# Issue positions of VectorE's weight merges, w_l and xl in the attention stage of a fused attention and gated-FFN kernel

## Chip, cores and metric

The kernel runs on one core of a Trainium2 chip. The metric is the device time of one execution in microseconds (us). An execution is taken apart by the hardware profiler; its engines are TensorE (PE for matmuls, PEld for weight loads), VectorE (DVE), ScalarE (ACT), GpSimd (POOL) and SyncE (SP), which here only issues DMAs.

## The reference

```
scores = (1/sqrt(64)) * q @ k.T          # B=4, H=12, S=448, D=64; causal mask
attn   = exp(scores - max) ; attn /= attn.sum + 1e-9
x      = (attn @ v) as 1792 x 768
xn     = x / sqrt(mean(x*x) + 1e-6) * rms_g
g, val = xn @ w_gate, xn @ w_val         # 768 x 1536 each
out    = (g * sigmoid(g) * val) @ w_out  # 1536 x 768
```

Everything is computed in float32 accuracy. Weights arrive as 64-bit floats and are turned into 32-bit ones on the chip.

## The kernel before

**Tiling.** The rows of x are cut into four groups: the first 256 queries of batches 0 and 1, those of batches 2 and 3, the next 128 queries of all batches and the last 64 (512, 512, 512 and 256 columns). The first group has 12 attention units (6 pairs of heads times two batches); its attention is the first stage, written out as rounds of six ticks. After it comes a loop over weight chunks `s` for each group: the FFN of one group runs while the attention of the next is threaded between its matmuls.

**A round of the first stage** (round r starts at tick 6r; `round_steps`, L425). Tick 0: the scores of unit r, eight matmuls (L180, called S), and four masked negated maxima on VectorE (L189). Tick 1: attn @ v of unit r-3 (L262, called AV) and its copy `xr` on VectorE (L271). Tick 2: the transposes of the first half of unit r-2 (L236, called T0), copied by ScalarE (`pt`, L242). Ticks 3 and 4: single FFN steps that are ready early (`ffn_part`, three matmuls L391 to L393: w_h times xh, w_h times xl, w_l times xh). Tick 5: the transposes of the second half (T1), copied by VectorE (`pt`, L240). At the end of tick 2 ScalarE's exponentials of unit r are issued (`exp0`), and at the end of tick 0 of the next round VectorE's reciprocal of the sums (L201) with GpSimd's four normalising multiplications (L197, `norm0`), which T0 and T1 read two rounds after the scores.

**Side work of the first stage.** `convert(s)` turns chunk s of the weights into 32 bits: ScalarE c0 (L352), GpSimd c1 (L353), VectorE c2 and c3 (L355 and L357, "the merges"), then a DMA that stores the chunk (L359). `split_w` makes w_h on ScalarE (L367) and w_l on VectorE (L369, even s) or GpSimd (L92, odd s). `split_x` makes xh on ScalarE (L306) and xl on VectorE (L307). `square` makes the squares and their sum `acc` on GpSimd (L92); the last sum goes through PE (`r_ps`, L314), ScalarE's root (L316) and VectorE's reciprocals (L319) into the FFN's first results.

**Order.** The schedule is written out by hand: each engine works through its instructions in the order in which the program issues them. `post(d, fn)` issues fn d ticks on, at the end of the tick before; `post(1, ...)` is the end of the same tick. `T` holds these delays, `LOAD`, `CONVERT` and `SPLIT` the ticks at which chunks are loaded, converted and split, `READY_W` and `READY_X` the ticks from which an early FFN step may be placed (only at ticks 3 and 4 of a round). What is posted for the same tick is issued in the order in which it was posted.

So before the change the VectorE queue around rounds 5 to 8 reads (max5 are the maxima of unit 5, pt3 the second copy of unit 3): `xr1 c2_0 pt2 c3_0 max5 rcp4 xr2 pt3 xl0 max6 rcp5 xr3 c2_1 wl0 pt4 c3_1 max7 rcp6 xr4 pt5 xl1 max8`.

Of the kernel before, what the change touches and what calls it, by code (L numbers as in the profile page):

```python
# [14 lines left out]
ALU = mybir.AluOpType  # L15
# [22 lines left out]
MASKED = -8.0e9  # L38


T = dict(c0=0, c1=1, c2=4, c20=9, c3=5, c30=10, c5=7, c50=14, exp=1, exp0=3, gt=1, hh=1, hl=4,
         ld=4, ld1=11, lv=5, norm0=7, norm1=2, r1=5, so=3, wl=2, wl0=8, xl=2, xl0=9)
LOAD = (4, 12, 24, 36, 48, 60, 74)
CONVERT = (20, 32, 44, 62, 76)
SPLIT = (33, 45, 57)

READY_W, READY_X = (45, 57, 68), (40, 52, 64, 76, 87)
WR = 4
WARM = [9, 0, 0, 2]
EXTRA = 4  # L50
# [5 lines left out]
def attention_ffn(ctx: ExitStack, tc: tile.TileContext, qk0, qk1, qk2, v, v2, w, g, out):  # L56
# [7 lines left out]
    nc = tc.nc  # L64
# [23 lines left out]
    def f32(ap):  # L88
        return ap.bitcast(F32)

    def pool_op(out_, a, op, b):
        nc.gpsimd.tensor_tensor(out_, a, b, op=op)  # L92
# [27 lines left out]
    def post(delay, fn):  # L120
        if delay <= 0:
            fn()
        else:
            later.setdefault(now[0] + delay, []).append(fn)
# [6 lines left out]
    xr, xh, xl, acc = {}, {}, {}, {}  # L131
# [6 lines left out]
    def load_qk(p):  # L138
        if p < len(UNITS):
            _, kind, _, _, row = UNITS[p]  # L140
            raw_qk[p] = raw.tile([P, 2, W], F32, tag="qk", name="qk_r")
            if kind == 2:
                nc.sync.dma_start(out=raw_qk[p], in_=qk2[row])
            else:
                nc.sync.dma_start(out=raw_qk[p][:, 0], in_=(qk0, qk1)[kind][row])
# [14 lines left out]
    def steps_s(p):  # L160
# [22 lines left out]
        def softmax(e, i, pss):  # L183
            o, wd = bl[i]
            ps, sp = pss[e][:, o: o + wd], pr["sp"][e][:, o: o + wd]
            n = len(bl) * e + i
            nm, sm, rs = (pr[m][:, n: n + 1] for m in ("nm", "sm", "rs"))
            mk = mask2 if kind == 2 else mask[:, 3 * P - wd:]
            nc.vector.tensor_tensor_reduce(  # L189
                out=sp, in0=ps, in1=mk, scale=nsc, scalar=3.0e38,  # L190
                op0=ALU.add, op1=ALU.min, accum_out=nm)
            post(T["exp" if p >= ENDS[0] else "exp0"], lambda: nc.scalar.activation(  # L192
                sp, sp, AF.Exp, bias=nm, scale=-1.0, accum_out=sm))
            if ENDS[0] + 3 <= p < ENDS[1]:
                pr["norms"].append(lambda: nc.scalar.mul(sp, sp, rs))
            else:
                pr["norms"].append(lambda: nc.gpsimd.tensor_scalar(  # L197
                    sp, sp, rs, 1.0, op0=ALU.mult, op1=ALU.mult))
# [6 lines left out]
        def step():  # L205
# [5 lines left out]
            for e in range(2):  # L211
                for i in range(len(bl)):
                    softmax(e, i, pss)
            post(T["exp" if p >= ENDS[0] else "exp0"], lambda: nc.scalar.activation(
                pr["sm"][:, :nb], pr["sm"][:, :nb], AF.Identity, bias=tiny))
            post(T["norm1" if kind else "norm0"], norm)
            post(2, lambda: load_qk(p + 4))
# [60 lines left out]
    def cols(b):  # L278
        return GROUPS[b][3]

    def square(b, c):
# [13 lines left out]
        if c == NP - 1:  # L295
            post(T["r1"], lambda: rms(b, acc[b]))
        waiting.append((b, c))

    def split_x():
        if not waiting:  # L300
# [5 lines left out]
        nc.scalar.mul(h, x, gc)  # L306
        post(T["xl0" if b == 0 and c < NP - 1 else "xl"], lambda: nc.vector.scalar_tensor_tensor(  # L307
            out=l, in0=x, scalar=gc, in1=f32(h), op0=ALU.mult, op1=ALU.subtract))
        xh[b, c], xl[b, c] = h, l

    def rms(b, sq):

        ps = ps_t.tile([P, W], F32, tag="t", name="r_ps")[:, : cols(b)]
        nc.tensor.matmul(ps, ones, sq, start=True, stop=True)  # L314
        r = rinv[b] = xx_p.tile([P, W], F32, tag="rms", name="rms", bufs=2)[:, : cols(b)]
        nc.scalar.activation(r, ps, AF.Sqrt, bias=eps, scale=1.0 / DM)  # L316
        for i in range(cols(b) // P):
            sl = slice(i * P, (i + 1) * P)
            nc.vector.reciprocal(r[:, sl], r[:, sl])  # L319
# [22 lines left out]
    def convert_ops(s):  # L342
        if s >= NU:
# [7 lines left out]
        return [  # L351
            (T["c0"], lambda: nc.scalar.mul(t, hf_, 2.0 ** -112)),  # L352
            (T["c1"], lambda: nc.gpsimd.tensor_scalar(  # L353
# [8 lines left out]
    def split_w(s):  # L362
        if s < NG * NU:
            t = wt[s]
            h = ws_p.tile([P, DM], F32R, tag="wh", name="w_h")
            l = ws_p.tile([P, DM], F32R, tag="wl", name="w_l")
            nc.scalar.copy(h, t)  # L367
            if s % 2 == 0 and (s < NU or cols(s // NU) < W):
                post(T["wl" if s > 1 else "wl0"], lambda: nc.vector.tensor_tensor(l, t, f32(h), op=ALU.subtract))  # L369
            else:  # L370
                post(T["wl"], lambda: pool_op(l, t, ALU.subtract, f32(h)))
            wt[s] = tuple(a.rearrange("p (k m) -> p k m", m=P) for a in (h, l))
# [75 lines left out]
    with tc.manual_schedule():  # L448
# [19 lines left out]

        for fs, at_ in ((load_w, LOAD), (lambda n: convert(n), CONVERT), (split_w, SPLIT)):
            for n, t_ in enumerate(at_):  # L470
                at_tick(t_, lambda fs=fs, n=n: fs(n))
# [13 lines left out]
        def convert(s):  # L485
            for d, op in convert_ops(s):
                post(d, op)
# [12 lines left out]
        for s in range(NG * NU):  # L500
            w_ = s // NU
            if s % NU == 0:
                at, goal = done, ends[w_ + 1] + 2 if w_ + 1 < NG else done
                if w_ + 2 == NG:
                    goal = ends[w_ + 1]
            if s + 7 < NU:
                post(T["ld"], lambda s=s: load_w(s + 7))
            if s + 6 >= NU:
                post(T["ld1"], lambda s=s: load_w(s + 6))
            for k0 in (0, 2, 4):  # L510
                ks = [k for k in (k0, k0 + 1) if (s, k) not in early]
                if ks:
                    ffn_part(s, ks)
                i = 3 * (s % NU) + k0 // 2 + 1
                while done < goal and (done - at) < (goal - at) * i / AT[w_]:
                    steps[done]()
                    done += 1
                if i >= 73:
                    split_x()
                if k0 == 0:  # L520
                    convert(s + 5)
                if k0 == (0 if s < 3 else 4):
                    split_w(s + 3)
                for fn in prep.pop(now[0], []):
                    fn()
                tick()
# [50 lines left out]
```

## Time and profile before

| | us |
|---|---|
| median of 3 runs | 722.12 (721.94 to 722.2) |
| the profiled execution, device time | 721.81 |
| its span, first to last instruction | 720.0 |
| PE busy in the span | 699.6 (97%) |
| VectorE, ScalarE, GpSimd busy | 418.6, 366.5, 415.0 |

The span begins at the first instruction. The first stage runs from about 5 us to about 68 us; from 75 us on PE has work nearly without a break. A row of a timeline gives start, duration, engine, source line, operation, output from input, shapes, and in brackets how long the engine was idle before it and what it waited for. Where consecutive operations of an engine overlap in their records, the distance from one start to the next is what an operation costs in a queue.

### The profile page before, as it was taken

To read this page: it belongs to the slowest core of one execution; us is meant where nothing else is said; L and a number is where in the kernel's file an instruction comes from. 1 tells how busy PE (TensorE), PEld (TensorE's weight loads), DVE (VectorE), ACT (ScalarE), POOL (GpSimd) and SP (SyncE) were. 2 spreads that over 40 slices of the span, in tenths; PEclk is the share of its full clock that TensorE was granted. 3 is DMA by queue.
4 is the path that set the end of the run, shared out by engine and by line. 5 is a ranking of instruction groups with operands and counts; after the bars stand their busy time and mean duration, and the time that the engine had idled before them with its cause. 6 is when DMAs were issued, how large, how long until landed. Compare 5 with 4: busy or idle time off the path is not lost.

```text
span 720.0 us, 11950 instructions
## 1 busy us (share of the span) xinstructions
PE 699.6 (97%) x4256; PEld 546.7 (76%) x4256; DVE 418.6 (58%) x857; ACT 366.5 (51%) x811; POOL 415.0 (58%) x349
## 2 busy tenths in 40 slices
PE   8778899999999999999999999999999999999998
PEld 6455667777777777777777777777777788899998
DVE  4976899999998454545454534234333442137752
ACT  6958777877856344434444444334344342235441
POOL 4988435466476454675576637266455563437763
PEclk9999999999999999999999999999999999999999
DMA  8746487778767433333334456353641423355553
GB/s 265 250 146 204 154 266 247 261 261 281 271 223 251 145 126 135 117 117 121 131 127 147 160 180 223 112 188 115 191 139 48 137 66 118 117 177 179 179 177 111
DMA packets 47307, 123.47 MB, mean 171 GB/s; under 512 B 5968, under 2 KB 12880, under 8 KB 47248
## 3 DMA queue, kind: packets, MB, share of 16 engines
q1 hardware_dynamic: 47248, 122.71, 51.5%
q8 instruction: 34, 0.56, 0.3%
q14 instruction: 25, 0.20, 0.1%
HBM read 103.03 MB, written 19.66 MB: 170 GB/s over the span
## 4 chain that ended last, share of the span: by engine, by line
PE 73%; DVE 11%; issue 5%; POOL 5%; ACT 4%; DMA 2%; POOLq 0%; DVEq 0%; ACTq 0%
PE m_ps L391 20%; PE m_ps L393 19%; PE m_ps L392 19%; PE av_ps L262 5%; PE s_ps L180 5%; PE t_ps L236 4%; DVE w L355 3%; POOL sp L197 2%; DVE w_c L357 2%; DMA w<-in_w 2%; DVE sp L189 2%; DVE w_l L369 1%; ACT sp L192 1%; POOL w L353 1%; ACT w_c L352 1%
## 5 line engine op out<-in xcount | busy, mean ns | idle before, releaser
L391 PE MATMUL m_ps<-xh,w_h 128*128 128x512 f32 (+1 forms) x576 | 221.7, 385 | 0.0
L92 POOL TENSOR_TENSOR w_l<-w_r,w_h 128x768 fp32r<-128x768 f32 x90 | 170.1, 1896 | 73.6 <-ACT w_h L367 45.1
L393 PE MATMUL m_ps<-xh,w_l 128*128 128x512 f32 (+1 forms) x576 | 210.6, 366 | 0.0
L392 PE MATMUL m_ps<-xl,w_h 128*128 128x512 f32 (+1 forms) x576 | 210.2, 365 | 0.0
L197 POOL TENSOR_SCALAR sp<-sp,rs 128x384 f32<-128x384 f32 (+3 forms) x132 | 84.0, 652 | 142.1 <-DVE rs L201 135.7
L192 ACT ACTIVATE sp<-sp,nm 128x128 f32<-128x128 f32 (+3 forms) x168 | 87.5, 524 | 71.7 <-DVE nm L189 71.2
L391 PEld LDWEIGHTS m_ps<-xh,w_h 128*128 128x128 f32 x576 | 109.2, 190 | 18.8 <-issue 3.8
L393 PEld LDWEIGHTS m_ps<-xh,w_l 128*128 128x128 f32 x576 | 109.0, 189 | 18.8
L367 ACT CAST w_h<-w_r 128x768 fp32r<-128x768 f32 x108 | 87.5, 826 | 64.2 <-DMA w_r<-w 39.9
L392 PEld LDWEIGHTS m_ps<-xl,w_h 128*128 128x128 f32 x576 | 109.5, 190 | 13.3
L391 PE MATMUL m_ps<-hh,w_h 128*128 128x512 f32 (+1 forms) x288 | 109.1, 379 | 0.0
L393 PE MATMUL m_ps<-hh,w_l 128*128 128x512 f32 (+1 forms) x288 | 105.0, 365 | 0.9 <-DVE w_l L369 0.9
L392 PE MATMUL m_ps<-hl,w_h 128*128 128x512 f32 (+1 forms) x288 | 104.8, 364 | 0.4 <-DVE hl L417 0.4
L240 DVE COPY pt<-t_ps 128x384 f32<-128x384 f32 (+1 forms) x84 | 49.8, 592 | 70.6 <-PE t_ps L236 70.5
L189 DVE CUSTOM_DVE_ANT_0 sp<-s_ps,mask 128x128 f32<-128x128 f32 (+3 forms) x168 | 67.2, 447 | 36.1 <-PE s_ps L180 34.5
L406 ACT ACTIVATE t_sb<-gr 128x512 f32<-128x512 f32 (+1 forms) x48 | 27.8, 578 | 110.5 <-DVE gr L405 110.5
L262 PEld LDWEIGHTS av_ps<-pt,v_r 128*64 128x64 f32 (+1 forms) x864 | 40.7, 137 | 48.3 <-issue 17.8
L262 PE MATMUL av_ps<-pt,v_r 128*64 128x128 f32 (+2 forms) x864 | 60.7, 269 | 11.8 <-DVE pt L240 6.7
L353 POOL TENSOR_SCALAR w<-w 128x768 f32<-128x768 f32 x36 | 44.0, 1223 | 42.1 <-ACT w_c L352 34.2
L236 PE MATMUL t_ps<-ident,sp 128*128 128x128 f32 (+1 forms) x384 | 63.0, 276 | 0.9 <-POOL sp L197 0.4
L393 PEld LDWEIGHTS m_ps<-hh,w_l 128*128 128x128 f32 x288 | 54.4, 189 | 10.3 <-DVE w_l L369 1.3
L236 PEld LDWEIGHTS t_ps<-ident,sp 128*128 128x128 f32 (+1 forms) x384 | 47.7, 138 | 18.7 <-POOL sp L197 3.0
(53 smaller groups left out, 878.5 us busy)
## 6 DMA issues: line engine op xcount, KB each, us to landing
w_r<-w SPq DMA_DIRECT2D x108, 384.0 KB, 3.8
w<-in_w SPq DMA_DIRECT2D x36, 768.0 KB, 5.1
w<-w_c SPq DMA_DIRECT2D x36, 384.0 KB, 2.8
qk_r<-in_qk SPq DMA_DIRECT2D x48, 256.0 KB, 3.1
qk_r<-in_qk SPq DMA_DIRECT2D x12, 512.0 KB, 3.6
v_r<-in_v SPq DMA_DIRECT2D x12, 448.0 KB, 6.1
out_t<-ob SPq DMA_DIRECT2D x18, 256.0 KB, 2.3
v_r<-in_v SPq DMA_DIRECT2D x24, 192.0 KB, 3.8
```

Of the source, the lines that this page charges most:

```text
L92: nc.gpsimd.tensor_tensor(out_, a, b, op=op)
L189: nc.vector.tensor_tensor_reduce(out=sp, in0=ps, in1=mk, scale=nsc, scalar=3.0e38, op0=ALU.add, op1=ALU.min, accum_out=nm)
L192: post(T["exp" if p >= ENDS[0] else "exp0"], lambda: nc.scalar.activation(sp, sp, AF.Exp, bias=nm, scale=-1.0, accum_out=sm))
L197: pr["norms"].append(lambda: nc.gpsimd.tensor_scalar(sp, sp, rs, 1.0, op0=ALU.mult, op1=ALU.mult))
L236: nc.tensor.transpose(ps[:kb, at: at + P], pr["sp"][e][:, o + kb * j: o + kb * (j + 1)], ident)
L240: nc.vector.tensor_copy(pt[:kb, :at], ps[:kb, :at])
L262: nc.tensor.matmul(av_ps[e * D: (e + 1) * D, p % 2, q0: q0 + n], raw_v[p][:kb, h, j, e, :], pr["pt", e][:kb, a0: a0 + n], start=(j == 0), ...
L353: (T["c1"], lambda: nc.gpsimd.tensor_scalar(hf_, hf_, 0.0, 1.0, op0=ALU.mult, op1=ALU.mult)),
L367: nc.scalar.copy(h, t)
L391: nc.tensor.matmul(ps, wh[:, k, :], mh, start=(first and k == ks[0]), stop=False)
L392: nc.tensor.matmul(ps, wh[:, k, :], ml, start=False, stop=False)
L393: nc.tensor.matmul(ps, wl[:, k, :], mh, start=False, stop=(last and k == 5))
```

## The change

The delays `c20` and `c30` of c2 and c3 (first five chunks) become 11 and 11 (from 9 and 10), that of the store `c50` 16 (from 14), that of w_l `wl0` 10 (from 8; it now also holds for chunk 2, which had `wl` = 2), that of xl `xl0` 10 (from 9). Chunk 4 is converted at tick 74 instead of 76, chunk 6 loaded at 76 instead of 74. READY_W moves by a tick for chunks 0 and 2; the early FFN steps keep their order. In the first stage c2, c3, w_l and xl are then all issued at the end of a tick 0, behind the maxima of that score step and ahead of the reciprocal posted for the same tick.

```
-T = dict(c0=0, c1=1, c2=4, c20=9, c3=5, c30=10, c5=7, c50=14, ...
-         ld=4, ld1=11, lv=5, norm0=7, norm1=2, r1=5, so=3, wl=2, wl0=8, xl=2, xl0=9)
-LOAD = (4, 12, 24, 36, 48, 60, 74)
-CONVERT = (20, 32, 44, 62, 76)
+T = dict(c0=0, c1=1, c2=4, c20=11, c3=5, c30=11, c5=7, c50=16, ...
+         ld=4, ld1=11, lv=5, norm0=7, norm1=2, r1=5, so=3, wl=2, wl0=10, xl=2, xl0=10)
+LOAD = (4, 12, 24, 36, 48, 60, 76)
+CONVERT = (20, 32, 44, 62, 74)
 SPLIT = (33, 45, 57)
-READY_W, READY_X = (45, 57, 68), (40, 52, 64, 76, 87)
+READY_W, READY_X = (46, 57, 69), (40, 52, 64, 76, 87)
...
-                post(T["wl" if s > 1 else "wl0"], lambda: nc.vector.tensor_tensor(l, t, f32(h), op=ALU.subtract))
+                post(T["wl" if s > 2 else "wl0"], lambda: nc.vector.tensor_tensor(l, t, f32(h), op=ALU.subtract))
```

The same stretch of the VectorE queue after the change: `xr1 pt2 max5 c2_0 c3_0 rcp4 xr2 pt3 max6 xl0 rcp5 xr3 pt4 max7 c2_1 c3_1 wl0 rcp6 xr4 pt5 max8 xl1`. Later in the stage: `max9 c2_2 c3_2 rcp8`, `max10 xl2 rcp9`, `max11 wl2 rcp10`, `max12 c2_3 c3_3 xl3 rcp11`, `max14 c2_4 c3_4 xl4 rcp13`. GpSimd's and PE's queues keep their order; on ScalarE c0 of chunk 4 and xh4 change places; on SP each store moves behind one load of v.

## Rows read from the trace of the kernel before

**Rows 1.** Stretches: length, busy us of PE, PEld, DVE, ACT, POOL; clock; DMA

```profile
75.20:720.00 644.80, 638.60 (x3853) 506.81 (x3853) 366.13 (x663) 309.72 (x630) 356.88 (x259) 1.00 0.50 167
...
17.80:68.10 50.30, 40.49 (x273) 25.90 (x273) 39.88 (x138) 39.18 (x134) 45.88 (x61) 1.00 0.62 203
```

**Rows 2.** Waits of PE from 12 to 76 us (total us, times, longest us)

```profile
PE av_ps L262 <- DVE pt L240: 6.7, 5, 1.8
```

**Rows 3.** VectorE in order of time: start us, duration us, what

```profile
17.86 0.95 DVE L355 SCALAR_TENSOR_TENSOR w<-w 128x768 int32<-128x768 int32 x1
18.73 0.55 DVE L240 COPY pt<-t_ps 128x384 f32<-128x384 f32 x1
...
20.15 0.28 DVE L189 CUSTOM_DVE_ANT_0 sp<-s_ps,mask 128x128 f32<-128x128 f32 x1
...
21.26 0.17 DVE L201 RECIPROCAL rs<-sm 128x4 f32<-128x4 f32 x1
21.35 0.39 DVE L271 COPY xr<-av_ps 128x256 f32<-128x256 f32 x1
21.66 0.54 DVE L240 COPY pt<-t_ps 128x384 f32<-128x384 f32 x1
22.13 0.74 DVE L307 SCALAR_TENSOR_TENSOR xl<-xr,g_sb,xh 128x512 fp32r<-128x512 f32 x1
22.79 0.28 DVE L189 CUSTOM_DVE_ANT_0 sp<-s_ps,mask 128x128 f32<-128x128 f32 x1
```

**Rows 4.** GpSimd in order of time, same columns

```profile
17.80 3.12 POOL L197 TENSOR_SCALAR sp<-sp,rs 128x128 f32<-128x128 f32 x4 [1.04 <-PE s_ps L180]
...
24.87 3.81 POOL L197 TENSOR_SCALAR sp<-sp,rs 128x128 f32<-128x128 f32 x4
...
29.77 1.28 POOL L92 TENSOR_TENSOR acc<-acc,sq 128x512 f32<-128x512 f32 x1
...
33.06 0.89 POOL L353 TENSOR_SCALAR w<-w 128x768 f32<-128x768 f32 x1
33.91 1.80 POOL L92 TENSOR_TENSOR w_l<-w_c,w_h 128x768 fp32r<-128x768 f32 x1
...
45.34 1.63 POOL L197 TENSOR_SCALAR sp<-sp,rs 128x128 f32<-128x128 f32 x4 [1.93 <-DVE rs L201]
```

**Rows 5.** VectorE in order of time, later in the first stage

```profile
33.99 2.54 DVE L355 SCALAR_TENSOR_TENSOR w<-w 128x768 int32<-128x768 int32 x1 [0.89 <-POOL w L353]
...
41.75 0.96 DVE L369 TENSOR_TENSOR w_l<-w_c,w_h 128x768 fp32r<-128x768 f32 x1 [2.21 <-ACT w_h L367]
...
55.93 0.29 DVE L189 CUSTOM_DVE_ANT_0 sp<-s_ps,mask 128x128 f32<-128x128 f32 x1 [0.40 <-POOL sp L197]
```

**Rows 6.** TensorE in order of time, last rounds of the first stage

```profile
54.86 0.93 PE L180 MATMUL s_ps<-qk_r 64*128 64x128 f32 x8
56.30 0.87 PE L262 MATMUL av_ps<-pt,v_r 128*64 128x256 f32 x8 [0.51 <-ACT pt L242]
57.10 0.55 PE L236 MATMUL t_ps<-ident,sp 128*128 128x128 f32 x3
...
58.87 0.49 PE L236 MATMUL t_ps<-ident,sp 128*128 128x128 f32 x3
59.29 0.93 PE L180 MATMUL s_ps<-qk_r 64*128 64x128 f32 x8
...
63.90 0.93 PE L180 MATMUL s_ps<-qk_r 64*128 64x128 f32 x8
```

**Rows 7.** TensorE behind the first stage

```profile
68.11 1.12 PE L314 MATMUL r_ps<-acc,ones 128*128 128x512 f32 x2 [1.59 <-POOL acc L92]
...
75.26 0.86 PE L262 MATMUL av_ps<-pt,v_r 128*64 128x256 f32 x6 [2.55 <-ACT pt L242]
```

**Rows 8.** ScalarE's square root of the norm

```profile
69.27 0.69 ACT L316 ACTIVATE rms<-r_ps,eps 128x512 f32<-128x512 f32 x1 [0.22 <-PE r_ps L314]
```

**Rows 9.** Clock in one stretch behind that (columns as in rows 1)

```profile
77.00:78.00 1.00, 1.00 (x6) 0.90 (x5) 0.43 (x1) 1.00 (x2) 0.49 (x1) 0.50 0.00 0
```

More of the change, by code (lines that the diff above doesn't have):

```diff
@@ L38 @@
 MASKED = -8.0e9
-T = dict(c0=0, c1=1, c2=4, c20=9, c3=5, c30=10, c5=7, c50=14, exp=1, exp0=3, gt=1, hh=1, hl=4,
-         ld=4, ld1=11, lv=5, norm0=7, norm1=2, r1=5, so=3, wl=2, wl0=8, xl=2, xl0=9)
-LOAD = (4, 12, 24, 36, 48, 60, 74)
-CONVERT = (20, 32, 44, 62, 76)
+T = dict(c0=0, c1=1, c2=4, c20=11, c3=5, c30=11, c5=7, c50=16, exp=1, exp0=3, gt=1, hh=1, hl=4,
+         ld=4, ld1=11, lv=5, norm0=7, norm1=2, r1=5, so=3, wl=2, wl0=10, xl=2, xl0=10)
+LOAD = (4, 12, 24, 36, 48, 60, 76)
+CONVERT = (20, 32, 44, 62, 74)
 SPLIT = (33, 45, 57)
-READY_W, READY_X = (45, 57, 68), (40, 52, 64, 76, 87)
+READY_W, READY_X = (46, 57, 69), (40, 52, 64, 76, 87)
 WR = 4
```

## Prediction

> **What bounds the kernel now.** I read the busy time by stretch first: from 75.2 us to the end PE works 638.6 of 644.8 us [rows 1], and its instructions there are not changed. So the change acts on the time at which that stretch begins, and little else. Then the stretch of the change: from 17.8 to 68.1 us PE is busy 40.5 of 50.3 us and GpSimd 45.9 [rows 1]. The waits of PE name one cause above all, the second copy pt on VectorE, 6.7 us in five waits [rows 2]; the order of VectorE's queue says why: c2, c3, w_l and xl stand ahead of pt and of the next maxima. That looks like 6.7 us to be had. But the timelines of VectorE and GpSimd, laid side by side, show a second thing. Four normalising multiplications of GpSimd take 1.63 us when nothing of VectorE's side work runs (the row at 45.34), and 3.81 us at 24.87, while c2, w_l and c3 run on VectorE. The other way round, c2 issued at 33.99 takes 2.54 us in place of 0.95, and ends 0.82 us behind the w_l that GpSimd had begun at 33.91 for 1.80 us [rows 3 to 5]. The two engines take turns: one whole operation waits for the other. Work that takes turns does not get shorter by changing places.
>
> Is there room? By the pitch of the rows, one set of norms is 1.6 us, a square with its sum 2.4 (the square lies between 28.68 and 29.77), c1 0.87, GpSimd's w_l 1.8, a merge or w_l of VectorE 0.87, an xl 0.66 [rows 3, 4]. In the new order there would be left, behind 19.4 us and up to r_ps at 68.11 [rows 7], 10 norms (16.0), a first square (1.0), five squares with sums (11.9), four c1 (3.5), one w_l of GpSimd (1.8), and on VectorE 10 merges, two w_l and six xl (8.7, 1.7, 4.0): 48.6 us of turns in 48.7 us, were all of it in turns. So what the change can save there is small, however many of PE's waits it moves.
>
> **The change, part by part.** Durations of a step in a queue, from start to start: four maxima 1.11, reciprocal 0.09, xr 0.31, pt 0.47 [rows 3]; scores to maxima 1.07 (54.86 to 55.93) [rows 5, 6]; AV 0.80, first transposes with two FFN steps 1.77, second transposes 0.42 [rows 6]. An FFN step alone is an estimate of 0.7 from these.
> Removed: in round 5 c2 leaves the place ahead of pt, c3 that ahead of the maxima. pt starts at 17.86 (before 18.73), the maxima at 18.33 (before 20.15) [rows 3].
> Added: c2 and c3 stand now ahead of the reciprocal. 18.33 + 1.11 + 1.74 gives 21.18 for it, against 21.26 [rows 3]: the maxima win 1.8 us and the reciprocal, which frees GpSimd's norms, nothing. That is the pattern of every such round: GpSimd is given its work no earlier, and PE's first transposes wait for it in place of AV waiting for pt.
> Carried on by hand with these pitches, the queues in the new order and whole operations in turns:
> - Round 6: xl between two norms, maxima 22.05, second transposes 24.25. Round 7: maxima 25.74 to 26.84, GpSimd's square first (it is free at 26.67), then c2, c3, w_l to 30.32. The early FFN step of this round needs that w_l for its third matmul: PE stands from 27.1 to 30.4, scores of unit 8 at 31.0. Before, w_l was there by then and nothing waited.
> - Round 8: xl behind the maxima holds the next FFN step in the same way; scores 9 at 35.6. Rounds 9 and 10: c2, c3 run to 39.7, scores 10 at 39.4. Here the change gains: w_l of chunk 2 is gone from a place where VectorE stood 2.21 us for ScalarE's w_h [rows 5]; reciprocal 9 comes at 42.6 in place of 45.0, and GpSimd, which was idle 1.93 us for it [rows 4], begins norms 9 at 44.2 in place of 45.34.
> - Rounds 11, 12: w_l to 49.0, scores 12 at 49.7, then c2, c3, xl to 54.2; norms 11 begin at 54.6. Scores 13 at 53.5, scores 14 at 58.25, against 59.29 [rows 6].
> - Round 14: maxima 59.3 to 60.4, c2, c3, xl to 62.95. The FFN step behind them needs this xl for its second matmul; before it lay ahead of the maxima. Then three transposes and one FFN step, and scores 15 at 64.6, against 63.90 [rows 6]: the 1.04 us won are lost, and 0.7 more.
> The end of the stage: from scores 15 follow on ScalarE exponentials, a copy and the root, 5.37 us before, of which 0.22 was a wait for r_ps [rows 6, 8]; 64.6 + 5.15 = 69.75 in place of 69.27. GpSimd's last sum comes at 67.85, against 68.1 [rows 7], so it is not the later one. Sum: +0.48 us for the root; the AV at 75.26 hangs on it through VectorE's reciprocals and ScalarE's tanh and pt [rows 7], and the rest on that AV.
>
> Costed at nothing: the store on SP goes two ticks down with c3 and behind one load of v; bounds 0 and a gain, since that load no longer waits for c3; I take 0 because PE waits for no load in the stage's list of waits, whose longest entry stands in [rows 2]. Load of chunk 6 two ticks later, conversion of chunk 4 two ticks earlier: covered by the 21 ticks from the load to the first use of chunk 6 in the loop behind the stage, 15 us at the 4.43 us of a round [rows 6]; if that cover went, the merges of that chunk would be late by what is missing. xh4 behind c0: 0.8 us late at most (one ScalarE operation, an estimate), hidden under the 2.4 us by which its xl is now further back. READY_W: no step changes place, 0.
>
> **A rule against the rows.** The norms at 24.87 grew by 2.2 us while 2.6 us of VectorE's operations ran [rows 3, 4]: about 0.2 us of each meeting is hidden. The Trainium skill, SBUF — State Buffer, section "SBUF: two separate sides", has it that whichever of the two engines starts first keeps the shared pair of ports for its whole instruction and the other fully blocks. The row at 33.99 agrees, the one at 24.87 agrees to four fifths. By the rule the sum stands as above; by the row at 24.87 some eight meetings would give back 1.6 us, which is the first rival.
>
> **The rivals.**
> - Overlap (faster). If each meeting of a GpSimd operation with merges hides 0.2 us and the gains of round 10 reach the end, the root comes 1.6 us earlier than in my walk and up to 2.5: 721.0 to 720.1, 720.5 us at the middle. For it: GpSimd's idle 1.93 us at 45.34 [rows 4]. Against: round 14 puts three operations in front of one FFN step whatever happened earlier. 0.21, of which 0.04 within 0.2% of before.
> - All of PE's waits go (faster): 722.1 - 6.7 = 715.4. Against it the 48.6 us of turns. 0.04.
> - The turn is lost (slower). In round 5 c2 is ready at 18.33 + 1.11 = 19.44, and GpSimd's square at 19.40, behind norms that began at 17.80 [rows 4] and have nothing to wait for any more. If the square goes first, the merges end 1 us later, and with them the reciprocal, the norms and in round 7 the w_l for which PE stands. In the same walk scores 15 come at 65.7 in place of 64.6: 1.1 more, 723.7. It decides from a lead of some 0.06 us: at 24.87 the norm that started 0.06 us ahead of c2 was not held up. 0.22, of which 0.05 within 0.2%.
> - The clock (slower). Behind PE's break of 2.55 us the granted clock was 0.50 in the stretch from 77 us [rows 7, 9], the lower of its two levels (1.2 in place of 2.4 GHz). PE's break in round 7 would be 3.3 us, longer than any in this stage now. A fall there would double the steps of about one round: 0.9 scores, 0.8 AV, 0.8 transposes, 0.7 an FFN step, 3.2 us, of which GpSimd's turns hide a half: 1.6 more, 724.2. 0.13.
>
> **How the numbers follow.** The profiled execution took 721.81, 0.31 under the median; 722.12 + 0.48 = 722.6 is the forecast, with 0.40. About 0.2% (1.44 us) is what a measurement here can tell from no change. Faster by more: 0.17 + 0.04 = 0.21. Within: 0.40 + 0.04 + 0.05 = 0.49. Slower: 0.17 + 0.13 = 0.30. The range goes down into the overlap (720.0) and up past the clock's case (724.6); what is left out is the 0.04, a part of the overlap and both slow cases at once, some 0.17.
>
> **What would show it.** Right: PE's waits for pt on VectorE shrink from 6.7 us to under 3, and in their place stand waits for GpSimd's sp (first transposes), for w_l in round 7 and for xl in round 14; reciprocal 4 at 21.2; scores 15 later than scores 14 by over 6 us (before 4.6). GpSimd's busy time in the stage stays within 2 us of 45.9. Wrong: GpSimd idle for reciprocals for over 4 us, or its norms all at 1.6 us and the stage's end over 1.5 us earlier; a granted clock under 1 before 60 us would say the last rival.

## The result, and the profile after

The changed kernel takes 725.72 us (median of 5 runs, 725.51 to 726.58), the kernel before 722.12 (median of 5, 721.34 to 722.97): a ratio of 1.0052 with a 95% interval of 1.0041 to 1.0064. The change costs 3.6 us. The forecast was 722.6 with a range up to 724.6, so the time lies above the range.

The profiled execution took 725.65 us (span 723.9). The stretches that answer to [rows 1], and two in which the clock fell; columns are start:end, length, busy us of PE, PEld, DVE, ACT, POOL, the granted clock, the DMA share and GB/s:

```profile
17.80:70.30 52.50, 43.23 (x283) 27.82 (x281) 41.02 (x137) 38.85 (x131) 37.58 (x60) 0.93 0.59 191
32.00:38.00 6.00, 5.72 (x25) 3.75 (x26) 3.44 (x15) 0.58 (x2) 4.69 (x8) 0.50 0.82 264
78.40:723.90 645.50, 639.67 (x3853) 507.54 (x3853) 366.38 (x663) 309.72 (x630) 357.60 (x259) 0.99 0.51 167
110.00:113.00 3.00, 3.00 (x9) 2.32 (x8) 3.00 (x3) 2.62 (x6) 2.85 (x2) 0.50 0.45 172
```

The part behind the stage has the same 3853 matmuls, and takes 645.5 us in place of 644.8. So 0.7 of the loss lies there, and the rest lies ahead of it. The kernel before does not have the clock fall at 110 us (its stretch from 110 to 113 us is at 1.00), but that this fall makes the 0.7 is not shown: in the profiles of all sixteen kernels of this document that part, counted from the AV at its head, takes 644.5 to 646.2 us, and the last section shows kernels with the fall that are short there and kernels without it that are longer. GpSimd is busy 37.6 us in the stage, where it was 45.9.

The waits between 12 and 76 us (for what, total us, times, longest), against [rows 2]:

```profile
POOL sp L197 <- DVE rs L201: 14.7, 8, 3.5
...
PE m_ps L393 <- DVE w_l L369: 4.6, 2, 3.8
...
PE m_ps L392 <- DVE xl L307: 1.8, 2, 1.6
```

PE's 6.7 us for pt are gone. In their place PE waits for w_l and for xl, 6.4 us together, and GpSimd for reciprocals, 14.7 us. The same line of the kernel before:

```profile
POOL sp L197 <- DVE rs L201: 5.0, 4, 1.9
```

TensorE, in order of time, against [rows 6] and [rows 7]: the w_l of round 7, scores 14, the xl of round 14, scores 15, `r_ps`, and the AV on which the rest hangs.

```profile
32.28 0.79 PE L393 MATMUL m_ps<-xh,w_l 128*128 128x512 f32 x1 [3.85 <-DVE w_l L369]
...
60.61 0.93 PE L180 MATMUL s_ps<-qk_r 64*128 64x128 f32 x8
...
65.64 0.50 PE L392 MATMUL m_ps<-xl,w_h 128*128 128x512 f32 x1 [1.60 <-DVE xl L307]
...
67.33 0.93 PE L180 MATMUL s_ps<-qk_r 64*128 64x128 f32 x8
...
70.31 1.13 PE L314 MATMUL r_ps<-acc,ones 128*128 128x512 f32 x2 [0.37 <-POOL acc L92]
...
78.48 0.86 PE L262 MATMUL av_ps<-pt,v_r 128*64 128x256 f32 x6 [2.58 <-ACT pt L242]
```

ScalarE's root, against [rows 8]:

```profile
72.49 0.69 ACT L316 ACTIVATE rms<-r_ps,eps 128x512 f32<-128x512 f32 x1
```

The root is 3.22 us later (72.49 against 69.27), and so is the AV (78.48 against 75.26): with the 0.7 us behind it that is the 3.9 us by which the span grew.

Where in the stage? A table of the starts of scores 6 and of the root, with the times from one step to the next, by the profiles; it is used for the experiments too. Each row is one execution, up to 1.3 us off the median of its kernel, so differences of a few tenths say nothing.

| kernel | scores 6 | 6 to 11 | 11 to 14 | 14 to 15 | 15 to root | root |
|---|---|---|---|---|---|---|
| before | 21.4 | 24.2 | 13.8 | 4.6 | 5.4 | 69.27 |
| after | 20.4 | 26.7 | 13.6 | 6.7 | 5.2 | 72.49 |
| e2, all xl back | 19.9 | 25.8 | 12.8 | 5.3 | 5.5 | 69.23 |
| e9, xl 0 to 3 back | 20.5 | 25.5 | 13.0 | 6.7 | 5.2 | 70.86 |
| e5, xl 4 back | 20.1 | 26.8 | 13.5 | 5.2 | 6.6 | 72.27 |
| e4, reciprocal first | 20.9 | 25.3 | 13.4 | 7.1 | 5.9 | 72.53 |
| e13, e4 with e5 | 20.5 | 25.6 | 13.4 | 4.5 | 6.7 | 70.75 |
| e8, w_l alone moved | 20.8 | 22.4 | 14.0 | 4.6 | 5.4 | 67.08 |

Rounds 6 to 11 lose 2.5 us and round 14 loses 2.1. And the two sides of VectorE's and GpSimd's queues, round 7, against [rows 3] and [rows 4]; VectorE first:

```profile
27.60 1.82 DVE L355 SCALAR_TENSOR_TENSOR w<-w 128x768 int32<-128x768 int32 x1
29.45 1.91 DVE L357 SCALAR_TENSOR_TENSOR w_c<-w_c,w 128x768 int32<-128x768 int32 x1
31.28 0.95 DVE L369 TENSOR_TENSOR w_l<-w_c,w_h 128x768 fp32r<-128x768 f32 x1
32.15 0.16 DVE L201 RECIPROCAL rs<-sm 128x4 f32<-128x4 f32 x1
```

GpSimd, round 7, and its norms behind the reciprocal of round 12:

```profile
27.56 1.04 POOL L92 TENSOR_TENSOR sq<-xr 128x512 f32<-128x512 f32 x1
28.68 1.86 POOL L92 TENSOR_TENSOR acc<-acc,sq 128x512 f32<-128x512 f32 x1
32.49 1.64 POOL L197 TENSOR_SCALAR sp<-sp,rs 128x128 f32<-128x128 f32 x4 [1.95 <-DVE rs L201]
...
56.97 1.63 POOL L197 TENSOR_SCALAR sp<-sp,rs 128x128 f32<-128x128 f32 x4 [3.51 <-DVE rs L201]
```

c2 was issued 0.04 us behind GpSimd's square and stood for it; then the sum `acc` slipped in between c2 and c3, and c3 stood again. Each took 0.9 us more than the 0.95 of an undisturbed one. Then GpSimd stood for the reciprocal behind them. The norms are now nearly all 1.63 us long: the turns that showed in [rows 4] as a stretched norm of 3.81 show here as idle time of GpSimd.

### The profile page after: what moved, and what is told of

Same layout as the page of the kernel before. It is cut to its first block, busy times and chain, and to the rows that moved or that the text cites. A ratio compares the mean times of both kernels' runs of the same rounds, so it can differ in the third digit from the quotient of the medians.

```text
span 723.9 us, 11947 instructions
## 1 busy us (share of the span) xinstructions
PE 702.2 (97%) x4256; PEld 548.6 (76%) x4256; DVE 420.3 (58%) x857; ACT 367.0 (51%) x811; POOL 407.8 (56%) x349
## 4 chain that ended last, share of the span: by engine, by line
PE 67%; DVE 1%; ACT 1%; DMA 1%; issue 0%; POOL 0%; DVEq 0%; POOLq 0%
PE m_ps L391 19%; PE m_ps L393 18%; PE m_ps L392 18%; PE av_ps L262 4%; PE s_ps L180 4%; PE t_ps L236 4%; DMA out_t<-ob 1%; PE r_ps L314 0%; DVE w_c L357 0%; DVE ob L399 0%; DVE w L355 0%; POOL acc L92 0%; ACT w_h L367 0%; ACT sp L192 0%; DVE sp L189 0%
## 5 line engine op out<-in xcount | busy, mean ns | idle before, releaser
L393 PE MATMUL m_ps<-xh,w_l 128*128 128x512 f32 (+1 forms) x576 | 211.7, 368 | 4.6 <-DVE w_l L369 4.6
L197 POOL TENSOR_SCALAR sp<-sp,rs 128x384 f32<-128x384 f32 (+3 forms) x132 | 74.7, 582 | 151.8 <-DVE rs L201 144.5
L393 PEld LDWEIGHTS m_ps<-xh,w_l 128*128 128x128 f32 x576 | 109.6, 190 | 24.3 <-DVE w_l L369 5.5
L192 ACT ACTIVATE sp<-sp,nm 128x128 f32<-128x128 f32 (+3 forms) x168 | 87.5, 523 | 71.4 <-DVE nm L189 70.8
L367 ACT CAST w_h<-w_r 128x768 fp32r<-128x768 f32 x108 | 87.3, 826 | 62.5 <-DMA w_r<-w 37.6
L393 PE MATMUL m_ps<-hh,w_l 128*128 128x512 f32 (+1 forms) x288 | 105.1, 365 | 0.6 <-DVE w_l L369 0.6
L353 POOL TENSOR_SCALAR w<-w 128x768 f32<-128x768 f32 x36 | 45.4, 1260 | 42.8 <-ACT w_c L352 36.2
L393 PEld LDWEIGHTS m_ps<-hh,w_l 128*128 128x128 f32 x288 | 54.3, 189 | 10.3 <-DVE w_l L369 1.0
```

Of the source, the lines that this page charges most:

```text
L197: pr["norms"].append(lambda: nc.gpsimd.tensor_scalar(sp, sp, rs, 1.0, op0=ALU.mult, op1=ALU.mult))
L353: (T["c1"], lambda: nc.gpsimd.tensor_scalar(hf_, hf_, 0.0, 1.0, op0=ALU.mult, op1=ALU.mult)),
L393: nc.tensor.matmul(ps, wl[:, k, :], mh, start=False, stop=(last and k == 5))
```

## The experiments

The experiments ran on three chips, each beside runs of the kernel before, whose medians were 722.42 to 722.92; so ratios are compared, not times. 0.001 is 0.7 us. Their times are medians, their ratios have 95% intervals in brackets. Theory A was that the wait for w_l in round 7, with the clock's fall behind it, is the loss. Its rivals were the late reciprocals (B) and the place of xl (C); theory D, formed from e2 to e8, is that two chains end together, the FFN steps that wait for xl and GpSimd's late norms.

**e1: w_l back, the rest as changed.**

```
-         ld=4, ..., wl=2, wl0=10, xl=2, xl0=10)
+         ld=4, ..., wl=2, wl0=8, xl=2, xl0=10)
...
-                post(T["wl" if s > 2 else "wl0"], ...
+                post(T["wl" if s > 1 else "wl0"], ...
```

> The changed kernel, but w_l of chunks 0 and 2 issued where they were before (delays 8 and 2), so that the early FFN step of round 7 no longer waits for w_l of chunk 0. Theory A (the 3.85 us wait for that w_l, with the fall of the clock behind it, is the main cost): 722.2 to 723.7 us, granted clock 1.00 from 30 to 40 us. Theory B (merges ahead of the reciprocals starve GpSimd's norms): the wait goes, but GpSimd still stands for reciprocals; 724.5 to 725.5. Theory C (the last xl, in round 14, costs most): within 0.5 us of 725.7.

725.62 us, 1.0046 (1.0029 to 1.0063). The wait for w_l is gone, and the loss stays, as theories B and C have it. PE's waits for xl are 1.8 us as in the changed kernel. But e1 is no clean test of theory A. A break and a fall of the clock remain, now in round 8, 0.72 from 32 to 38 us:

```profile
32.88 1.92 PE L262 MATMUL av_ps<-pt,v_r 128*64 128x256 f32 x8 [1.93 <-ACT sm L214]
```

And e1 also takes back the w_l of chunk 2, whose move is a gain by itself (e12 below): its scores 10 are at 41.02, 1.8 us ahead of the changed kernel's, and then round 10 takes 7.6 us in place of 4.3. The w_l of chunk 0 alone was not taken back in any run.

**e2: all xl back.**

```
-xl0=10
+xl0=9
```

> The changed kernel, but xl issued ahead of the maxima as before (delay 9). Theory C: PE's wait of 1.60 us for xl in round 14 goes and scores 15 come 1.6 us earlier or more; 723.5 to 724.2 us. Theories A and B: the clock still falls near 32 us; not below 724.7.

722.72 us, 1.0001 (0.9991 to 1.0011): the loss is gone, and by more than theory C forecast. Yet this kernel has the very wait that theory A named, and a stretch of low clock, as its wait (total, times, longest) and its stretch from 30 to 40 us show:

```profile
PE m_ps L393 <- DVE w_l L369: 4.0, 1, 4.0
```

```profile
30.00:40.00 10.00, 8.61 (x45) 5.54 (x45) 6.26 (x22) 4.60 (x15) 8.33 (x12) 0.66 0.46 158
```

Its scores 11 come 1.3 us ahead of those of the changed kernel, its scores 14 are 2.1 ahead, and its root is at 69.23. So a break of 4.0 us in mid-stage and a fall of the clock behind it do not by themselves make the loss, and theory A is out. That they cost nothing is not shown: the gain of 0.0015 that w_l brings when it alone is moved (e8) is missing from e2, and some of it may have gone into them.

**e3: PE kept at work through the wait for w_l**, with 15 matmuls whose one operand is zero, ahead of L393 of the first early step.

```
+            if s == 0 and k == 0:
+                for _ in range(15):
+                    nc.tensor.matmul(ps, zero, mh, start=False, stop=False)
```

> The changed kernel with 15 matmuls of zeros by xh added into the open sum of the early FFN step of round 7, ahead of the matmul that waits for w_l (they add zero, about 3.4 us of work at full clock, less than the break). PE is busy through the break, w_l comes no earlier. Clock theory: clock 1.00 from 30 to 40 us, and the time falls by 1 to 2 us, to 723.7 to 724.7. If the wait itself is all that costs: within 0.4 us of 725.7.

726.35 us, 1.0047 (1.0029 to 1.0064), no better. The low clock did not vanish but moved: 0.89 from 30 to 40 us, 0.66 from 37 to 42, behind a wait of 1.9 us for xl in round 8. So e3 cannot say what the stage would be without a fall.

**e4: the reciprocal ahead of the merges.**

```
-            post(T["norm1" if kind else "norm0"], norm)
+            if kind:
+                post(T["norm1"], norm)
+            else:
+                later.setdefault(now[0] + T["norm0"], []).insert(0, norm)
```

> The changed kernel, but the reciprocal of the sums of the unit before is issued right behind the maxima, ahead of c2, c3, w_l and xl of the same tick. Theory B: GpSimd's idle time for reciprocals (1.7 to 3.5 us in five rounds) goes, its norms meet the merges again, and the time falls by 1.5 us or more, to 724.2 or less. Theory A: w_l of chunk 0 comes as late or later (the norms take turns with the merges), the wait and the fall of the clock stay; 725 to 727.

725.27 us, 1.0034 (1.0021 to 1.0047). GpSimd's waits for reciprocals fall from 14.7 to 6.5 us, and the ratio falls by 0.0018, 1.3 us where theory B forecast 1.5 or more; the intervals of the two ratios overlap. PE waits 2.0 us for xl in round 14 all the same, and scores 15 come 7.1 us behind scores 14:

```profile
64.74 0.50 PE L395 MATMUL m_ps<-xl,w_h 128*128 128x512 f32 x1 [1.98 <-DVE xl L310]
```

The root of e4 is at 72.53, where the changed kernel has it, though `r_ps` no longer waits for GpSimd. The 0.85 us by which its profiled execution is shorter lie behind the stage. So within the stage this cure alone shows nothing.

**e5: only xl of unit 4 back** (round 14).

```
+        post(9 if b == 0 and c == 4 else ...
```

> The changed kernel, but the xl of column 4 alone is issued ahead of the maxima of round 14 as before (delay 9 for c = 4). Theory C1 (the loss lies in round 14: an FFN step waits there for the xl that now stands behind c2 and c3, and scores 15 with the root of the norm hang on it): 722.5 to 723.5 us, like the run with every xl moved back; scores 15 come 5.3 us behind scores 14 in place of 6.7. Theory C2 (the xl of rounds 6 to 12 cost as well): 724.2 to 725.2, since scores 14 stay near 60.6.

725.37 us, 1.0037 (1.0024 to 1.005), by the ratio what theory C2 forecast. Round 14 is cured, 5.2 us from scores 14 to 15, but the root moves by 0.2 us only. TensorE's row for `r_ps` and ScalarE's for the root say why:

```profile
70.16 2.07 PE L314 MATMUL r_ps<-acc,ones 128*128 128x512 f32 x2 [1.86 <-POOL acc L92]
```

```profile
72.27 0.69 ACT L316 ACTIVATE rms<-r_ps,eps 128x512 f32<-128x512 f32 x1 [0.86 <-PE r_ps L314]
```

The last sum of GpSimd is as late as in the changed kernel, PE stands 1.86 us for it, and `r_ps` runs at a clock of 0.51 behind that break (2.07 us for 1.13). The root then waits for `r_ps`. Two chains end at nearly the same time: scores 15 with ScalarE's exponentials, and GpSimd's norms with its last square and sum.

**e6, e7, e8: one part alone on the kernel before**: xl (`xl0=10`), the merges (`c20=11, c30=11, c50=16`), w_l (`wl0=10`, `s > 2`, READY_W).

> The kernel before with xl alone moved behind the maxima (delay 10). Theory C: most of the loss is here too, 724.2 to 725.7 us, with scores 15 over 6 us behind scores 14. If xl costs only together with merges ahead of it in the same place: 722.0 to 723.2; in round 14 c2 and c3 stay three ticks behind the maxima here, so that xl is issued 1.7 us earlier.

> The kernel before with c2 and c3 of the first five chunks (and the store behind them) moved behind the maxima, nothing else. Theory C: no loss, 722.0 to 723.2 us. Theory B (merges ahead of reciprocals starve GpSimd): 724 us or more, with GpSimd's waits for reciprocals at 10 us or more and scores 14 late.

> The kernel before with w_l of chunks 0 and 2 alone moved behind the maxima. Theory A: PE stands for w_l in round 7, 723.5 us or more. Theory C: it gains the 2.21 us for which VectorE stood for w_h or is hidden; 721.0 to 723.0.

722.85 us, 1.0001 (0.9992 to 1.0011) for xl; 722.73, 1.0006 (0.999 to 1.0021) for the merges; 721.3, 0.9985 (0.9975 to 0.9995) for w_l. No part alone loses; w_l alone gains.

**e11: w_l and xl, no merges** (e8 with `xl0=10`).

> The kernel before with w_l of chunks 0 and 2 and all xl moved, the merges c2 and c3 left where they were. If xl costs only together with merges that stand ahead of it: c2 and c3 lie elsewhere, root near that of w_l alone (67.1 to 68.0) and 721.0 to 722.0. Rival, xl behind the maxima costs by itself when the rounds run early (w_l moved): root at 69 or later, 722.5 to 725.

722.69 us, 0.9998 (0.9985 to 1.0011): the rival's time, and with 68.97 nearly its root, though the interval reaches into the other forecast. With e1, e2 and the changed kernel all eight combinations are measured. In every row but the third the two kernels differ in xl alone; e1 also has the changed LOAD, CONVERT and READY_W, and e7 has not:

| moved | without xl | with xl | price of xl |
|---|---|---|---|
| nothing else | 1 | 1.0001 (e6) | 0.0001 |
| w_l | 0.9985 (e8) | 0.9998 (e11) | 0.0013 |
| merges | 1.0006 (e7) | 1.0046 (e1) | 0.0040 |
| merges and w_l | 1.0001 (e2) | 1.0052 (after) | 0.0051 |

The loss is a product of two parts: xl costs 2.9 to 3.7 us once the merges stand behind the same maxima, about 0.9 with w_l moved (the intervals of e8 and e11 overlap), and nothing by itself. The last row, whose two kernels differ in nothing else, carries this reading.

**e9 and e10: which xl?** e9 has xl of units 0 to 3 back, e10 those of units 3 and 4.

```
+        post((9 if c < 4 else 10) if b == 0 and c < NP - 1 ...      (e9)
+        post((10 if c < 3 else 9) if b == 0 and c < NP - 1 ...      (e10)
```

> The changed kernel with xl of units 0 to 3 back at a delay of 9 ticks and only xl of unit 4 left at 10. Theory D, two chains that end together: without the four early xl the reciprocal of round 12 comes as early as with all xl back (its norms at about 54.8 us), scores 14 start at about 58.5 us in place of 60.6, but round 14 keeps its FFN step waiting for xl, so scores 15 follow 6.5 to 7 us later and the root comes at 70.0 to 70.8: 723.0 to 724.5. Rival, the xl of round 14 is the whole loss: 725.3 to 726.2 as with the whole change. Rival, only the early xl cost anything: 722.2 to 723.0.

> The changed kernel with xl of units 3 and 4 back at 9 ticks, and xl of units 0 to 2 left at 10. Theory D as rounds 12 and 14 have it: round 12 loses the xl ahead of reciprocal 11 and round 14 the xl ahead of which its FFN step stands; root at 69.2 to 70.0, 722.3 to 723.5. Rival, the loss is already made by rounds 6 to 10 (scores 11 at 47.0 in place of 45.7): root at 71 or later and 724.5 to 725.7.

e9: 723.78 us, 1.0012 (1.0 to 1.0023). e10: 724.62 us, 1.0023 (1.0013 to 1.0032). With e2, e5 and the changed kernel that is a ladder: none back 1.0052, unit 4 back 1.0037, units 3 and 4 back 1.0023, all back 1.0001. Each step down is 1 to 1.6 us, with intervals that overlap from one step to the next save at the last; e9 gives the single price of unit 4 from the other side, 0.0011. So theory D had e9's time right (root 70.86, a hair above its 70.0 to 70.8), but e10 it had wrong: the time is its rival's and the ratio lies between the two, so xl of units 0 to 2, in rounds 6 to 10, hold 0.0022 of the loss, where theory D had given them next to none. In the profile of e10 scores 6 were already 2.0 us late (22.4) from a wait of 2.0 us and a low clock in the rounds before the change acts, so its root of 72.33 is not compared.

What xl does in an early round is seen in round 8. VectorE of the changed kernel, maxima, xl, reciprocal; then the same stretch of e9, where xl is ahead of the maxima:

```profile
35.44 0.29 DVE L189 CUSTOM_DVE_ANT_0 sp<-s_ps,mask 128x128 f32<-128x128 f32 x1 [1.13 <-PE s_ps L180]
...
36.55 0.75 DVE L307 SCALAR_TENSOR_TENSOR xl<-xr,g_sb,xh 128x512 fp32r<-128x512 f32 x1
37.22 0.17 DVE L201 RECIPROCAL rs<-sm 128x4 f32<-128x4 f32 x1
```

```profile
34.09 1.26 DVE L307 SCALAR_TENSOR_TENSOR xl<-xr,g_sb,xh 128x512 fp32r<-128x512 f32 x1
35.30 0.29 DVE L189 CUSTOM_DVE_ANT_0 sp<-s_ps,mask 128x128 f32<-128x128 f32 x1
...
36.42 0.17 DVE L201 RECIPROCAL rs<-sm 128x4 f32<-128x4 f32 x1
```

VectorE has to wait for the scores ahead of its maxima anyhow: 1.13 us idle in the changed kernel. In e9 xl lies in that gap and costs the maxima nothing. Behind the maxima it stands ahead of the reciprocal, which comes at 37.22 in place of 36.42, and GpSimd is idle for it. GpSimd's norms in round 8 of the changed kernel, then of e9:

```profile
37.56 1.63 POOL L197 TENSOR_SCALAR sp<-sp,rs 128x128 f32<-128x128 f32 x4 [0.82 <-DVE rs L201]
```

```profile
34.78 2.25 POOL L92 TENSOR_TENSOR w_l<-w_c,w_h 128x768 fp32r<-128x768 f32 x1
37.01 1.62 POOL L197 TENSOR_SCALAR sp<-sp,rs 128x128 f32<-128x128 f32 x4
```

The norms of e9 start 0.55 us earlier, less than its reciprocal's 0.80: there xl took a turn with GpSimd's w_l, which is 1.81 us long in the changed kernel.

**e13 and e14: both cures at once.** e13 is e4 with xl of unit 4 back as in e5; e14 is e4 with all xl back as in e2.

> The changed kernel with both cures at once: the reciprocal of each round issued ahead of the merges, and xl of unit 4 alone back at 9 ticks. Theory D (two chains end together; each cure alone gave 0.4 to 0.5 us because the other chain stayed late): both together give far more than the sum, root at 69.2 to 70.2, 722.3 to 723.6. Rival, the cures simply add: 724.6 to 725.2, root at 71 or later.

> The changed kernel with the reciprocal ahead of the merges and all xl back at 9 ticks: only merges and w_l stand behind the maxima. If GpSimd's waits for reciprocals are what eats the gain of moving w_l: as w_l alone, 720.8 to 721.8, root at 67 to 68. Rival, the merges in turn with GpSimd's norms set the pace whatever the order: 722.3 to 723.2, root at 69.

e13: 723.88 us beside 722.92 for the kernel before, 1.0008 (0.9998 to 1.0018). As a time that lies between the two forecasts, and so does its root of 70.75. As a ratio it is theory D's, whichever median of the kernel before on record (722.12 to 722.92) the forecast times are set against. By the sum of the two cures (0.0018 and 0.0015) it would be 1.0019. So the two cures together take nearly the whole loss. That they give more than their sum is likely but not shown by the times, as 1.0019 lies a hair outside the interval and the two cures have their own. The roots say the same: e4 moved it by nothing, e5 by 0.2 us, both together by 1.7. e14: 1.0002 (0.9993 to 1.0011): the rival's time, with a root of 70.35 that is later than either forecast. GpSimd waits only 4.0 us for reciprocals, and still none of w_l's gain is left. What takes it back was not isolated. PE still waits 3.1 us for w_l in round 7, with the clock at 0.72 from 32 to 38 us, and in the last round VectorE's xl meets GpSimd's square and takes 1.57 us (from 64.77; before 0.93), which holds up the maxima behind it: they begin 1.9 us behind scores 15, before 1.1.

**e12: w_l of chunk 2 alone.**

```
+        post({0: 8, 2: 10}.get(s, T["wl"]), ...      (kernel before, READY_W of chunk 2 at 69)
```

> The kernel before with w_l of chunk 2 alone moved behind the maxima of round 11 (chunk 0's w_l stays). If the gain of moving w_l comes from VectorE's 2.21 us wait for w_h of chunk 2, this one move brings it all: 720.8 to 721.8, root at 67 to 68. Rival, it comes from chunk 0's w_l in round 7: 722.2 to 722.8, root at 69.

721.42 us, 0.9989 (0.9978 to 1.0). Root at 67.31, that of e8 at 67.08. By the root this one operation carries nearly all of e8's gain; by the times its interval just reaches no change. The profiled executions of both are about 1 us shorter than their medians. VectorE of e8, where it stood idle for 2.21 us in [rows 5]:

```profile
45.30 1.97 DVE L369 TENSOR_TENSOR w_l<-w_c,w_h 128x768 fp32r<-128x768 f32 x1
```

It no longer waits for w_h, only for its turn. e8 is faster than both kernels, by 0.0015 than the one before. Its root is 2.19 us earlier and its profiled execution 1.46 us. Some of the difference is in TensorE's row for the AV behind the stage, which takes 1.54 us at a clock of 0.50, where [rows 7] has 0.86; it need not be all, as from the start of that AV to the end e8 takes 0.8 us more than the kernel before, but e12, which has the same row, only 0.4:

```profile
73.06 1.54 PE L262 MATMUL av_ps<-pt,v_r 128*64 128x256 f32 x6 [2.53 <-ACT pt L242]
```

## Why the prediction was wrong

The walk that the prediction made by hand through the queues, against the profile of the changed kernel (starts, us):

| | scores 8 | scores 9 | scores 10 | scores 12 | scores 13 | scores 14 | scores 15 | root |
|---|---|---|---|---|---|---|---|---|
| walk | 31.0 | 35.6 | 39.4 | 49.7 | 53.5 | 58.25 | 64.6 | 69.75 |
| measured | 33.6 | 38.9 | 42.8 | 51.9 | 55.8 | 60.6 | 67.3 | 72.49 |

- **What bounds the kernel**: right. The root moved by 3.22 us and everything behind it by as much; only 0.7 us of the loss arose later, no more than that part differs from kernel to kernel.
- **Round 5**: the maxima began at 19.00 and not at 18.33, since this execution's second AV stood 1.6 us for v; the merges then ran undisturbed, and the reciprocal came at 22.32 (walk 21.18). Right in its pattern: it came no earlier.
- **Round 7, the first half of the step that failed**: the place was right, the size wrong. The walk let GpSimd's square go first and then c2, c3 and w_l in one run to 30.32. The maxima began 0.8 us later than in the walk (26.50), and the sum that follows the square took a turn of 1.1 us between c2 and c3, which the walk did not have; so w_l ended at 32.23. The wait was 3.85 us in place of 3.3. The "turn lost" rival had its lost turn in round 5, where in the event nothing met; the turn was lost here.
- **The clock, the second half**: the forecast put it at nothing, and as a rival gave it 0.13. It came true, 0.50 from 32 to 38 us, behind a break of 3.85 us. With the late w_l it makes the 3.3 us by which scores 9 are late against the walk (38.9 for 35.6). The case of both at once is the one that the range left out.
- **Behind scores 9 the walk holds in sum**: 34.15 us to the root forecast, 33.56 measured; its largest miss there is 1.2 us too many from scores 10 to 12. Round 12 is right: 4.9 us from scores 12 to the norms in the walk, 5.06 measured (56.97). So the walk went wrong ahead of scores 9, in those two terms.
- **But these two terms alone do not make a loss**: e2 has both, with scores 9 at 38.36, and no loss. It takes 30.87 us from scores 9 to its root and so makes good what the rounds before lost; the changed kernel, with xl behind the maxima, does not.
- **xl** is what the walk gave no price of its own. It had xl in its queues, where an FFN step waits for it (rounds 8 and 14) and ahead of the reciprocal (round 12), and of these round 14 was right: 6.35 us from scores 14 to 15 forecast, 6.7 measured, with a wait of 1.60. In round 8 no FFN step waited for it. But no rival asks what the rest of the change would do with xl left in the gap in which VectorE waits for scores, and the runs show that the loss hangs on this: 1.0052 with xl moved, 1.0001 without. By the ladder the four early xl cost some 2.9 us (1.0052 less 1.0012), unit 4 some 0.8 to 1.1.
- **The turns**: 48.6 us of turns in 48.7 us was taken as leaving little to gain. It is no bound: e8 does the same operations, only two merges (1.7 us) of them ahead of 19.4, and its `r_ps` starts at 65.91, 46.5 us behind that; so not all of them run in turns. It was read as a price too, as if GpSimd would be kept at work: it then stood 14.7 us for reciprocals. A sum of turns does not say how long the chain through reciprocals makes a stage. The stated test, GpSimd busy within 2 us of 45.9, failed with 37.6 in a stretch longer by 2.2 us, and two of the stated signs of being wrong came: GpSimd idle for reciprocals for over 4 us, and a clock under 1 before 60 us. Of the signs of being right PE's waits for w_l and xl came; those of its first transposes for GpSimd's sp did not.
- **The rule of the Trainium skill**, SBUF — State Buffer, section "SBUF: two separate sides", that the engine that starts first keeps the shared ports and the other is blocked: c3 at 29.45 agrees. It ended 0.82 us after the sum's end at 30.54, against 0.95 for a whole merge that nothing disturbs.
- **READY_W, the store, load and conversion**: costed at nothing. e8 moves READY_W without a loss, and e2 has all of them at 1.0001 with a gain of w_l that is missing; what hides there, if anything, is within the 0.0016 between e8 and e2 and was not taken apart.

The end of the stage had less slack than the walk said: GpSimd's last sum was not the later chain, as forecast, but only by the 1.05 us between the end of `r_ps` at 71.44 and the root at 72.49, and e5 shows it take over.

What stays open: what the wait for w_l in round 7 and the fall behind it cost, since no run takes back the w_l of chunk 0 alone; and why the first three xl cost 1.6 us when the merges are moved and nothing when they are not. In the kernel before GpSimd waits 5.0 us for reciprocals and not 14.7, so a later reciprocal is often hidden behind work that GpSimd still has; that is argued from the waits, and no run isolates it.

## What to carry to other kernels

Before moving side work on an engine's queue, look at the gap that it lies in: an operation that fills a wait for another engine's result costs its own queue nothing, and the same operation behind that result stands ahead of whoever needs it next, here the reciprocal that starts GpSimd's round. Price a move together with the others that land in the same place: three moves that each cost nothing, or gain, cost 3.6 us together. When two chains end together, a cure of one shows little; try both before a theory is dropped.

## What the hardware showed that was not expected

A break and a low clock in mid-stage need not show at the end. e2 lost 4.0 us of PE's time at one point and ran at a mean of 0.66 from 30 to 40 us, and ended where the kernel before ended; e7 had a break of 2.00 us and 0.83 over the same stretch, and no loss beyond its interval either. The likely reason is that the chain through VectorE and GpSimd was the later one, as PE stood 1.59 us for GpSimd's last sum in e2 as in the kernel before; no run isolates it.

The clock fell to 0.50, the lower of its two levels (1.2 in place of 2.4 GHz), behind breaks of 3.85 us at 32 us and of 1.77 us ahead of the AV at 108.75; in the kernel before a break of 1.67 us ahead of the same AV was followed by none. The stretch from 104 to 130 us, of the changed kernel and of e2:

```profile
104.00:130.00 26.00, 24.23 (x116) 18.19 (x115) 25.90 (x42) 18.49 (x40) 11.76 (x9) 0.93 0.76 265
```

```profile
104.00:130.00 26.00, 24.56 (x115) 19.26 (x116) 25.86 (x41) 20.52 (x49) 13.41 (x9) 0.93 0.74 251
```

e2 has the fall too, behind a break of 1.71 us and with a root where the kernel before has it. So this fall does not come from the later root alone. Nor does the length of the break tell which way it goes: ahead of the same AV, 1.71 us in e7 and 1.73 us in e6 were followed by none, 1.68 us in e10 by a fall (0.52 from 110 to 113 us). What it costs is not shown. From the AV at the head of the part behind the stage to the end, the changed kernel takes 645.42 us and e2 645.18, with the fall, and the kernel before 644.74, without; but e10, with it, takes 644.78, and e11, without, 646.05.
